# Cosine attention and a highway FFN: 112-row chunks scheduled by the framework, against 128-row lanes of three tokens in one fixed order

## The chip, the cores and the metric

One Trainium2 chip, one of its cores. The metric is the device time of one execution in microseconds (us). The engines are named as in the profile: PE (TensorE, matrix products; PEld its weight loads), DVE (VectorE), ACT (ScalarE), POOL (GpSimd), SP (SyncE, which here only issues DMAs). "PSUM" is the memory that PE writes, "SBUF" the working memory.

## The reference

Eight batches, twelve heads, 448 tokens, 64 elements per head. Attention with q and k divided by their norms, then a highway layer over the joined heads:

```python
q_n = q / (norm(q, axis=-1) + 1e-6);  k_n = k / (norm(k, axis=-1) + 1e-6)
scores = q_n @ k_n.T / tau                       # tau = 0.1; (8, 12, 448, 448)
attn = exp(scores - max) / (sum + 1e-9)
x = (attn @ v) as (8*448, 12*64) = (3584, 768)
H = maximum(x @ w_h, 0);  T = sigmoid(x @ w_t + b_t)     # w_h, w_t: 768 x 768
out = T * H + (1 - T) * x
```

All inputs and the output are float32.

## The kernel before

A batch has six pairs of neighbouring heads (2 pr, 2 pr + 1). The 448 tokens of a head lie on 112 partitions with four tokens each (chunk c = token 4p + c), so that all tiles have 112 rows.

*Norms and loads.* `emit_A` loads q and k of a pair (L92, 256-byte pieces, by SP), squares both on POOL (L97, 1024 elements a row) and sums them on DVE (L104). `emit_rsqrt` turns the sums into 1/norm on DVE by a bit trick and two Newton steps (L125 to L144): for batch 0 pair by pair, later once a batch.

*Transposes.* `emit_B` multiplies q and k by 1/norm on POOL (L152), transposes the eight 112 x 128 blocks on PE (L157), copies them out of PSUM on DVE (L164), loads v (L168) and casts it to fp16 on ACT (L174); a 65th column holds 2.0, so that the product with v also yields twice the sum of the exps.

*Scores.* `emit_qkt` computes k times q for two chunks of both heads (L186: contraction 64, the two heads in the upper and the lower half of the array), into two PSUM tiles of two banks each, and takes the exp of 896 elements at a time on ACT (L194) with the immediate scale 1/tau.

*Values.* `emit_av` multiplies exps with v: 16 products of 65 columns a head (L210), then a reciprocal and a scaling on DVE (L221, L222) into the batch's x tile, which so holds x/2.

*FFN.* For each quarter of the tokens `emit_xt` transposes x (L236) and copies it out (L242). `emit_ffn_quarter` runs six products of 384 columns (L257) for each half of w_h and of w_t, the bias as a seventh (L265), a tanh on ACT for the gate (L273), and max(H, 0) - x on DVE (L276). `emit_ffn_final` ends with two DVE operations a half (L293, L301) and a store (L309).

*Order.* The loops at the end of the kernel emit attention of batch b, FFN of batch b - 1 and the preparation of batch b + 1 interleaved; batch 0's preparation and the weights (L73, cast on DVE at L76) come first. The framework's scheduler places the instructions on the engines by these positions, with raised priority for the copies out of PSUM. All DMAs are issued by SP.

Of the kernel before, what the change touches and what calls it, by code (L numbers as in the profile page):

```python
# [15 lines left out]

@with_exitstack
def kernel(
# [12 lines left out]

    B, NH, S, D = q.shape
    P = 112
    NC = S // P
    NPAIR = NH // 2
    DM = NH * D
    CC = DM // 128
    MH = DM // 2
    inv_tau = 1.0 / float(tau)  # L40

    assert (B, NH, S, D) == (8, 12, 448, 64)

    const = ctx.enter_context(tc.tile_pool(name="const", bufs=1))
    wraw_p = ctx.enter_context(tc.tile_pool(name="wraw", bufs=1))
    qkraw_p = ctx.enter_context(tc.tile_pool(name="qkraw", bufs=7))
    qksq_p = ctx.enter_context(tc.tile_pool(name="qksq", bufs=3))
    nrm_p = ctx.enter_context(tc.tile_pool(name="nrm", bufs=2))
    qkn_p = ctx.enter_context(tc.tile_pool(name="qkn", bufs=4))
    qt_p = ctx.enter_context(tc.tile_pool(name="qt", bufs=4))  # L50
    vraw_p = ctx.enter_context(tc.tile_pool(name="vraw", bufs=3))
    vp_p = ctx.enter_context(tc.tile_pool(name="vp", bufs=4))
    expt_p = ctx.enter_context(tc.tile_pool(name="expt", bufs=4))
    xb_p = ctx.enter_context(tc.tile_pool(name="xb", bufs=2))
    xt_p = ctx.enter_context(tc.tile_pool(name="xt", bufs=2))
    ffns_p = ctx.enter_context(tc.tile_pool(name="ffns", bufs=4))
    outst_p = ctx.enter_context(tc.tile_pool(name="outst", bufs=4))

    sT_p = ctx.enter_context(tc.tile_pool(name="sTpool", bufs=2, space=bass.MemoryType.PSUM))
    pb1_p = ctx.enter_context(tc.tile_pool(name="pb1pool", bufs=2, space=bass.MemoryType.PSUM))  # L60
    ffnp_p = ctx.enter_context(tc.tile_pool(name="ffnpool", bufs=2, space=bass.MemoryType.PSUM))

    ident = const.tile([P, P], FP16)
    make_identity(nc, ident)
    w_h_f = const.tile([128, CC, DM], FP16)
    w_t_f = const.tile([128, CC, DM], FP16)
    bth = const.tile([128, DM], FP16)
    ones_row = const.tile([128, 128], FP16)

    def emit_weights():  # L70
        for w_src, w_dst in ((moe_w_h, w_h_f), (moe_w_t, w_t_f)):
            w_raw = wraw_p.tile([128, CC, DM], FP32, tag="wraw")
            nc.sync.dma_start(  # L73
                w_raw[:, :, :], w_src.rearrange("(cc p) m -> p cc m", p=128)
            )
            nc.vector.tensor_copy(w_dst[:, :, :], w_raw[:, :, :])  # L76

        bt_raw = wraw_p.tile([1, DM], FP32, tag="btraw")
        nc.sync.dma_start(bt_raw[:1, :], moe_b_t)
        nc.vector.memset(bth[:, :], 0.0)  # L80
        nc.vector.memset(ones_row[:, :], 0.0)
        nc.vector.tensor_single_scalar(bth[:1, :], bt_raw[:1, :], 0.5, ALU.mult)
        nc.vector.memset(ones_row[:1, :], 1.0)

    out_v = out.rearrange("(b p ic) m -> b ic p m", b=B, ic=NC)

    st = {}

    def emit_A(b, pr):
        qk_raw = qkraw_p.tile([128, 2, NC, 2, D], FP32, name="qk_raw")  # L90
        for t, src in enumerate((q, k)):
            nc.sync.dma_start(  # L92
                qk_raw[:P, t],
                src[b, 2 * pr : 2 * pr + 2].rearrange("h (p c) d -> p c h d", c=NC),
            )
        qk_sq = qksq_p.tile([128, 2, NC, 2, D], FP16, name="qk_sq")
        nc.gpsimd.tensor_mul(qk_sq[:P], qk_raw[:P], qk_raw[:P])  # L97

        if pr == 0:
            n2 = nrm_p.tile([128, NPAIR, 2, NC, 2], FP16, name="n2")  # L100
            st["n2", b] = n2
        n2 = st["n2", b]
        with nc.allow_low_precision(reason="norm^2 in fp16 (rel err 5e-4)"):
            nc.vector.reduce_sum(n2[:P, pr], qk_sq[:P], axis=AX.X)  # L104
        st["qk_raw", b, pr] = qk_raw

    def emit_rsqrt(b, prs=None):
        n2 = st["n2", b]
        NE = NPAIR * 2 * NC * 2
        if prs is None:  # L110
            if ("rs", b) not in st:
                st["rs", b] = nrm_p.tile([128, NE], FP32, name="yy")
            x32 = nrm_p.tile([128, NE], FP32, name="x32")
            yy = st["rs", b]
            tt_ = nrm_p.tile([128, NE], FP32, name="tt_")
            n2s = n2[:P].opt()
        else:
            if ("rs", b) not in st:
                st["rs", b] = nrm_p.tile([128, NE], FP32, name="yy")
            NE = 16  # L120
            x32 = nrm_p.tile([128, NE], FP32, name="x32p")
            yy = st["rs", b][:, prs * 16 : (prs + 1) * 16]
            tt_ = nrm_p.tile([128, NE], FP32, name="tt_p")
            n2s = n2[:P, prs].opt()
        nc.vector.tensor_copy(x32[:P], n2s)  # L125
        nc.vector.tensor_single_scalar(
            yy[:P].bitcast(I32), x32[:P].bitcast(I32), 1, ALU.arith_shift_right
        )
        nc.vector.tensor_scalar(
            out=yy[:P].bitcast(I32),  # L130
            in0=yy[:P].bitcast(I32),
            scalar1=-1.0,
            scalar2=float(0x5F3759DF),
            op0=ALU.mult,
            op1=ALU.add,
        )
        for _ in range(2):
            nc.vector.tensor_mul(tt_[:P], yy[:P], yy[:P])
            nc.vector.tensor_mul(tt_[:P], tt_[:P], x32[:P])
            nc.vector.tensor_scalar(  # L140
                out=tt_[:P], in0=tt_[:P], scalar1=-0.5, scalar2=1.5,
                op0=ALU.mult, op1=ALU.add,
            )
            nc.vector.tensor_mul(yy[:P], yy[:P], tt_[:P])  # L144

    def emit_B(b, pr):
        qk_raw = st.pop(("qk_raw", b, pr))
        rs = st["rs", b].rearrange("p (pr t c h) -> p pr t c h", pr=NPAIR, t=2, c=NC)
        qkn = qkn_p.tile([128, 2, NC, 2, D], FP16, name="qkn")
        for t in range(2):  # L150
            in1 = rs[:P, pr, t].unsqueeze(3).to_broadcast([P, NC, 2, D])
            nc.gpsimd.tensor_mul(qkn[:P, t], qk_raw[:P, t], in1)  # L152

        qkT = pb1_p.tile([128, 2, 512], FP16, name="qkT", tag="pb1")
        for t in range(2):
            for c in range(NC):
                nc.tensor.transpose(  # L157
                    qkT[:, t, c * P : (c + 1) * P],
                    qkn[:P, t, c],
                    ident[:P, :P],  # L160
                )
        qkt = qt_p.tile([128, 2, S], FP16, name="qkt")
        with tc.high_priority(offset=300):
            nc.vector.tensor_copy(qkt[:, :, :], qkT[:, :, 0:S])  # L164
        st["qkt", b, pr] = qkt

# [186 lines left out]
    for h in range(NH):  # L353
        ffn_slot(B - 1, h)
# [35 lines left out]
```

## Time and profile before

| what | value |
|---|---|
| median of three runs | 487.74 us |
| lowest, highest | 483.55, 488.44 us |
| span of the profiled execution | 485.1 us |
| instructions in it | 8592 |
| PE busy | 369.8 us (76%), 3328 matmuls |
| DVE busy | 309.2 us (64%) |
| ACT busy | 225.6 us (47%) |
| POOL busy | 206.4 us (43%) |
| mean granted PE clock | 0.903 |
| read from memory, written | 37.75 MB, 11.01 MB |
| DMA packets under 512 bytes | 131873 of 137034 |

The profile is of one execution; it lists its span from the first to the last instruction, and no device time of its own beside it. Busy time of PE counts each matmul from its start to its modelled end, so that matmuls that follow each other closely overlap. "Idle before, releaser" behind a group is the time for which its engine stood idle just before it, and the instruction that ended most of that. In the tables by stretch, the number in brackets is a count of instructions.

### The profile page before, as it was taken

The page shows a single profiled execution, that of the slowest core. Times are in us where ns is not written, and L with a number is a line of the kernel's source. Part 1 is how long each engine was busy: PE and PEld are TensorE (multiplying, and loading weights), DVE is VectorE, ACT ScalarE, POOL GpSimd, SP SyncE. Part 2 cuts the span into 40 slices and gives each one's busy share as a digit, 9 for nine tenths or more (in the row PEclk, how much of TensorE's full clock was granted, in tenths as well). Part 3 has the DMA queues.
Part 4 walks back from the last instruction along what each step waited for, and adds up shares of the span by engine and source line. Part 5 has one row for each costly group of instructions (what it writes and reads, how often), then busy time and mean ns, then how long its engine had stood idle before and what let it go on. Part 6 is the DMA issues. An engine that isn't in the chain of part 4 may idle for free.

```text
span 485.1 us, 8592 instructions
## 1 busy us (share of the span) xinstructions
PE 369.8 (76%) x3328; PEld 240.3 (50%) x3328; DVE 309.2 (64%) x661; ACT 225.6 (47%) x305; POOL 206.4 (43%) x294
## 2 busy tenths in 40 slices
PE   0553843796848777889887988887887999898995
PEld 0212502563425355556565655555555666465673
DVE  3656555458647787774978584858568555445674
ACT  2330632343525444644755473475356556645511
POOL 3663376833674175738363833374327122000000
PEclk9999999998978597876999797899789799789999
DMA  9980596941627335743663662356241122000122
GB/s 160 198 235 1 190 207 107 171 71 49 145 56 143 85 91 119 144 103 85 137 135 88 139 144 59 86 125 130 63 103 49 40 77 68 28 30 30 30 64 79
DMA packets 137034, 49.31 MB, mean 102 GB/s; under 512 B 131873, under 2 KB 131873, under 8 KB 136994
## 3 DMA queue, kind: packets, MB, share of 16 engines
q1 hardware_dynamic: 136994, 48.77, 46.2%
q8 instruction: 26, 0.43, 0.4%
q14 instruction: 14, 0.11, 0.1%
HBM read 37.75 MB, written 11.01 MB: 101 GB/s over the span
## 4 chain that ended last, share of the span: by engine, by line
PE 46%; DVE 24%; POOL 12%; ACT 6%; issue 6%; DMA 4%; SPq 0%; POOLq 0%; ACTq 0%
PE pt L257 24%; PE sT L186 9%; PE u L210 9%; POOL qkn L152 8%; DVE th1a L293 6%; DVE outst L301 5%; DVE n L104 5%; POOL qk_sq L97 5%; DMA qk_raw<-in_k_dram 4%; ACT expt L194 4%; PE qkT L157 3%; ACT tt L273 2%; DVE xTb L242 2%; PE pt L265 1%; DVE qkt L164 1%
## 5 line engine op out<-in xcount | busy, mean ns | idle before, releaser
L194 ACT ACTIVATE expt<-sT 112x896 f16<-112x896 f32 x192 | 166.2, 916 | 92.8 <-PE sT L186 73.2
L257 PEld LDWEIGHTS <-xTb 128*112 128x112 f16 x768 | 100.4, 143 | 58.7 <-DVE xTb L242 23.6
L186 PE MATMUL sT<-qkt 64*112 64x448 f16 x384 | 105.2, 434 | 25.8 <-ACT expt L194 25.1
L152 POOL TENSOR_TENSOR qkn<-qk_raw,yy 112x512 f16<-112x512 f32 x96 | 100.0, 1070 | 54.6 <-DVE yy L144 35.3
L257 PE MATMUL pt<-w_h_f,xTb 128*112 128x384 f16 x384 | 97.5, 394 | 14.4 <-DVE xTb L242 14.1
L97 POOL TENSOR_TENSOR qk_sq<-qk_raw 112x1024 f16<-112x1024 f32 x48 | 94.1, 1968 | 29.2 <-DMA qk_raw<-in_k_dram 21.7
L210 PEld LDWEIGHTS <-expt 112*128 112x128 f16 x1536 | 70.1, 108 | 46.2 <-issue 21.8
L210 PE MATMUL u<-vp,expt 112*128 112x65 f16 x1536 | 80.2, 210 | 16.1 <-DVE xbach L222 12.5
L104 DVE TENSOR_REDUCE n<-qk_sq 112x16 f16<-112x1024 f16 x48 | 58.1, 1212 | 40.6 <-POOL qk_sq L97 29.2
L257 PE MATMUL pt<-w_t_f,xTb 128*112 128x384 f16 x384 | 77.1, 329 | 3.3 <-DVE hmx L276 3.1
L174 ACT CAST vp<-v_raw 112x512 f16<-112x512 f32 x48 | 29.8, 621 | 99.3 <-PE u L210 81.5
L157 PE MATMUL qkT<-ident,qkn 112*128 112x112 f16 x384 | 35.2, 244 | 46.2 <-POOL qkn L152 43.6
L293 DVE SCALAR_TENSOR_TENSOR th1a<-tt,hmx 112x384 f16<-112x384 f16 x64 | 48.9, 764 | 28.6 <-ACT tt L273 28.3
L186 PEld LDWEIGHTS <-qkt 64*112 64x112 f16 x384 | 31.3, 140 | 63.1 <-issue 55.6
L273 ACT ACTIVATE tt<-pt 112x384 f16<-112x384 f32 x64 | 31.4, 491 | 61.6 <-PE pt L265 61.6
L276 DVE SCALAR_TENSOR_TENSOR hmx<-pt,xbach 112x384 f16<-112x384 f32 x64 | 35.2, 552 | 34.4 <-PE pt L257 34.4
L157 PEld LDWEIGHTS <-qkn 112*128 112x128 f16 x384 | 27.4, 113 | 57.0 <-POOL qkn L152 49.1
L340 POOL MEMSET expt<- 112x16 f16 x96 | 11.5, 126 | 102.6 <-PE u L210 65.8
L301 DVE SCALAR_TENSOR_TENSOR outst<-xbach,th1a 112x384 f32<-112x384 f16 x64 | 45.7, 715 | 1.0
L164 DVE COPY qkt<-qkT 128x896 f16<-128x896 f16 x48 | 29.8, 620 | 21.6 <-PE qkT L157 13.3
L222 DVE SCALAR_TENSOR_TENSOR xbach<-u,rd 112x256 f16<-112x256 f32 x96 | 40.2, 420 | 1.9
L221 DVE RECIPROCAL rd<-u 112x4 f32<-112x4 f32 x96 | 17.0, 177 | 28.5 <-PE u L210 28.5
(56 smaller groups left out, 125.0 us busy)
## 6 DMA issues: line engine op xcount, KB each, us to landing
qk_raw<-in_q_dram SPq DMA_DIRECT2D x48, 224.0 KB, 4.5
qk_raw<-in_k_dram SPq DMA_DIRECT2D x48, 224.0 KB, 4.7
v_raw<-in_v_dram SPq DMA_DIRECT2D x48, 224.0 KB, 3.7
out_dram<-outst SPq DMA_DIRECT2D x32, 336.0 KB, 2.9
w_raw<-in_moe_w_h_dram SPq DMA_DIRECT2D x1, 2304.0 KB, 10.1
w_raw<-in_moe_w_t_dram SPq DMA_DIRECT2D x1, 2304.0 KB, 9.2
bt_raw<-in_moe_b_t_dram SPq DMA_DIRECT2D x1, 3.0 KB
```

The lines of the kernel that those rows point to most:

```text
L97: nc.gpsimd.tensor_mul(qk_sq[:P], qk_raw[:P], qk_raw[:P])
L104: nc.vector.reduce_sum(n2[:P, pr], qk_sq[:P], axis=AX.X)
L152: nc.gpsimd.tensor_mul(qkn[:P, t], qk_raw[:P, t], in1)
L157: nc.tensor.transpose(qkT[:, t, c * P : (c + 1) * P], qkn[:P, t, c], ident[:P, :P],)
L186: nc.tensor.matmul(sTs[hh][:P, jj, 0:S], lhsT=qkt[hh * D : (hh + 1) * D, 1, jc * P : (jc + 1) * P], rhs=qkt[hh * D : (hh + 1) * D, 0, 0:S] ...
L194: nc.scalar.activation(st["expt", b, 2 * pr + hh][:P, 2 * g * S : (2 * g + 2) * S].rearrange("p (j s) -> p j s", j=2), sTs[hh][:P, :, 0:S] ...
L210: nc.tensor.matmul(u[:, ic, 0 : D + 1], lhsT=expt[:P, jc * S + ic * P : jc * S + ic * P + 128], rhs=vp[:P, jc, hh], start=(jc == 0), stop= ...
L222: nc.vector.scalar_tensor_tensor(out=xb[:P, pr, :, hh, :], in0=u[:P, :, 0:D], scalar=0.0, in1=rd[:P, :].unsqueeze(2).to_broadcast([P, NC, D]),
L257: nc.tensor.matmul(pt[:P, :], lhsT=xT[:, cc, ic * P : (ic + 1) * P], rhs=w_f[:, cc, mh * MH : (mh + 1) * MH], start=(cc == 0), stop=(cc == ...
L273: nc.scalar.activation(tt[:P, mh], pt[:P, :], AF.Tanh)
L293: nc.vector.scalar_tensor_tensor(out=th1a[:P, mh], in0=tt[:P, mh], scalar=1.0, in1=hmx[:P, mh], op0=ALU.add, op1=ALU.mult,)
L301: nc.vector.scalar_tensor_tensor(out=outst[:P, mh * MH : (mh + 1) * MH], in0=xg, scalar=2.0, in1=th1a[:P, mh], op0=ALU.mult, op1=ALU.add,)
```

## The change

The kernel is rewritten; the arithmetic is the same up to where factors are applied.

*Layout.* The first 384 tokens of a head lie on 128 partitions ("lanes") of three tokens each, and the last 64 are a tail. Heads n and n + 6 form a pair: their rows sit side by side, and their two tails (64 + 64 rows) share one 128-row tile.

*Loads.* q and k of a whole batch come in one DMA each, issued by POOL, which converts to fp16 on the way (1536 pieces of 768 bytes); the weights likewise. v, the tails and, for batch 0, the first two pairs (as float32) come by SP and ACT. Batch b + 1's loads stand in POOL's stream behind some q scalings of the batch before.

*Norms.* Squares on DVE in fp16, folded 64 to 32 to 16 by additions and then summed; Newton steps for a batch at once. Only q is multiplied by 1/norm (POOL). k is left unscaled: its 1/norm times 1/tau is a column of numbers, one for each partition, that the exp takes as its scale.

*Attention of a pair.* Nine transposes of 128 columns (three of q, three of k, two of q's tail, one of k's tail, laid out as a block diagonal of the two heads) into one PSUM bank, one copy of 1024 elements; six score products of 448 columns and six exps of 448; one product of 512 columns for the tail keys of both heads and one exp of 512; then 24 + 8 products of 65 columns, one reciprocal and one scaling of 448. The PSUM tiles are one bank each: four for scores (ring S), four for all else (ring B).

*FFN of a batch.* Three full tiles of 128 tokens, and a half tile with the 64 tails: its 64 rows are split over two column tiles of the array, the two halves of the 768 outputs side by side in one bank. Gate: tanh of half on ACT, gate scale and product on DVE in fp16, the final sum on POOL (on DVE for the last two tiles).

*Order.* Every operation is entered in a plan with assumed costs. A list `ORDER` of 1907 numbers is walked by `Plan.follow`, which gives each operation a start and its buffers; they are then emitted by start, and the framework keeps that order on each engine and adds the waits. Operations marked `port` (DVE products, copies in SBUF, POOL work) are kept apart in the plan only.

```diff
-        qk_sq = qksq_p.tile([128, 2, NC, 2, D], FP16, name="qk_sq")
-        nc.gpsimd.tensor_mul(qk_sq[:P], qk_raw[:P], qk_raw[:P])
...
-            nc.vector.reduce_sum(n2[:P, pr], qk_sq[:P], axis=AX.X)
...
-            nc.gpsimd.tensor_mul(qkn[:P, t], qk_raw[:P, t], in1)
...
-        for hh in range(2):
-            nc.scalar.activation(
-                st["expt", b, 2 * pr + hh][:P, 2 * g * S : (2 * g + 2) * S].rearrange(
-                    "p (j s) -> p j s", j=2
-                ),
-                sTs[hh][:P, :, 0:S],
-                AF.Exp,
-                scale=inv_tau,
-            )
...
+    NR = dict(qr=3, kr=3, qt=2, kt=2, kb=2, vr=2, vt=2, vp=2, sq=3, f1=2, f2=2, n2=2, rs=3, qn=3, kp=3,
+              qtn=2, qT=3, E=3, Et=3, rd=2, x=3, xT=3, tt=3, hm=3, gt=3, gg=3, os=4, S=4, B=4)
...
+    def main_src(t, b):
+        return t[b, :, 0 : 3 * 128, :].rearrange("h (l c) d -> l h (c d)", c=NCH)
...
+            if p1 - p0 == 6:
+                eng.dma_start(dst[:, :, :], main_src(src, b))
...
+                if onact:
+                    nc.scalar.activation(d, a, AF.Square)
+                else:
+                    nc.vector.tensor_mul(d, a, a)
...
+            lambda: nc.vector.tensor_add(v("f1"), v("sq")[:, :, :, 0:32], v("sq")[:, :, :, 32:64]),
+            lambda: nc.vector.tensor_add(v("f2"), v("f1")[:, :, :, 0:16], v("f1")[:, :, :, 16:32]),
+            lambda: nc.vector.reduce_sum(
...
+            nc.gpsimd.tensor_mul(
+                R("qn", s).rearrange("l c ab d -> l ab c d"),
+                rows(0, b, p, p + 1).rearrange("l ab (c d) -> l ab c d", c=NCH),
+                rcol(b, 0, p).unsqueeze(3).to_broadcast([128, 2, NCH, D]),
...
+            nc.vector.tensor_copy(R("kp", s).rearrange("l c ab d -> l ab c d"),
+                                  rows(1, b, p, p + 1).rearrange("l ab (c d) -> l ab c d", c=NCH))
...
+                for ab in range(2):
+                    qT = R("qT", s)[64 * ab : 64 * ab + 64]
+                    nc.tensor.matmul(R("S", 7 * s + 2 * c + ab)[:, 0:448],
+                                     lhsT=qT[:, 512 + 128 * c : 640 + 128 * c],
+                                     rhs=qT[:, 64 * (1 - ab) : 64 * (1 - ab) + 448],
+                                     start=True, stop=True)
...
+                    nc.scalar.activation(
+                        R("E", s)[:, c, 512 * ab : 512 * ab + 448], R("S", 7 * s + 2 * c + ab)[:, 0:448], AF.Exp,
+                        scale=rcol(b, 1, p)[:, ab, c : c + 1])
...
+                            for h in range(2):
+                                nc.tensor.matmul(
+                                    P[64 * h : 64 * h + 64, 0:MH],
+                                    lhsT=xT[:, cc % 3, 64 * (cc // 3) : 64 * (cc // 3) + 64],
+                                    rhs=w_[:, cc, MH * h : MH * h + MH], start=st, stop=(cc == CC - 1))
...
+        op("DVE", f"gt {g}", lambda: nc.vector.tensor_scalar(
+            out=R("gt", g)[:, 0:W], in0=R("tt", g)[:, 0:W], scalar1=0.5, scalar2=0.5, op0=ALU.mult, op1=ALU.add),
...
+        op("DVE", f"gg {g}", lambda: nc.vector.tensor_mul(
+            R("gg", g)[:, 0:W], R("gt", g)[:, 0:W], R("hm", g)[:, 0:W]), o, l, key + 0.3,
...
+        eng, en = (nc.vector, "DVE") if last else (nc.gpsimd, "POOL")
...
+        op(en, f"out {g}", lambda: eng.tensor_add(R("os", g)[:, 0:W], xall(), R("gg", g)[:, 0:W]), o, l, key + 0.3,
...
+    plan = pl.follow(ORDER)
+    with nc.allow_low_precision(reason="fp16 operands of the products, squares and gates as given"):
+        with tc.manual_schedule():
+            for o in plan:
+                o.fn()
```

How the six pairs of a batch are entered, with the keys that say where an operation belongs:

```python
for p in range(NP):
    s = base + p                  # base = 6 * b
    qnorm(b, p, s - 1.5)
    turn(b, p, s - 0.8)           # transposes, copy out of PSUM
    vcast(b, p, s - 0.5)
    scores(b, p, s)
    attend(b, p, s + 0.7)
for i in range(4):
    ffn(b, i, base + 7.0 + 1.6 * i)
```

856 lines of the change are left out of this document (581 added, 275 removed), and 78 rows, old and new, of the table ORDER.

## The prediction

> **What bounds the kernel now.** I read the page's head and its chain of waits first, then the table of stretches, cut where the FFN's first matmul starts (101 us) and where batch 7 has only its FFN and a few heads left (443 us).
>
> ```profile
> span 485.1 us, 8592 instructions
> ...
> PE 46%; DVE 24%; POOL 12%; ACT 6%; issue 6%; DMA 4%; SPq 0%; POOLq 0%; ACTq 0%
> ```
>
> ```profile
> core 0: us, PE busy (x) PEld busy (x) DVE busy (x) ACT busy (x) POOL busy (x), PEclk, DMA share, GB/s
> 0.00:101.00 101.00, 48.94 (x373) 26.96 (x374) 54.84 (x135) 33.58 (x41) 57.43 (x72) 1.00 0.84 159
> 101.00:443.00 342.00, 286.25 (x2662) 188.14 (x2660) 230.11 (x474) 178.73 (x244) 148.70 (x220) 0.87 0.39 91
> 443.00:485.00 42.00, 34.58 (x296) 25.23 (x294) 24.25 (x53) 13.31 (x21) 0.22 (x2) 0.98 0.17 53
> ```
>
> The chain has no single owner: it hops between PE, DVE and POOL. There are three regimes. In the first 101 us PE issues 373 of its 3328 matmuls; DMA (0.84) and POOL are the busy ones. In the middle 342 us (seven batches, 48.9 us each) PE shows 286 us busy, but that counts the latency of each matmul. What PE must really spend is the spacing of matmuls that stand queued. Four merged rows of the timeline show it:
>
> ```profile
> 251.23 0.83 PE L257 MATMUL pt<-w_t_f,xTb 128*112 128x384 f16 x4
> 252.06 0.56 PE L157 MATMUL qkT<-ident,qkn 112*128 112x112 f16 x8
> ...
> 252.92 0.67 PE L210 MATMUL u<-vp,expt 112*128 112x65 f16 x16
> 253.52 0.58 PE L186 MATMUL sT<-qkt 64*112 64x448 f16 x3
> ```
>
> Taking off the last one's own duration (0.33, 0.24, 0.21, 0.41) and dividing by the steps between starts gives 0.167 us for 384 columns, 0.046 for a transpose of 112, 0.031 for one of 65, and 0.09 for 448 columns where two half-height products run side by side. With the counts of the middle and of the end:
>
> ```profile
> L257 PE MATMUL pt<-w_h_f,xTb 128*112 128x384 f16 x313 | 84.1, 409 | 13.0 <-DVE xTb L242 12.7
> L186 PE MATMUL sT<-qkt 64*112 64x448 f16 x307 | 77.1, 409 | 19.5 <-ACT expt L194 18.9
> L257 PE MATMUL pt<-w_t_f,xTb 128*112 128x384 f16 x312 | 63.0, 330 | 2.9 <-DVE hmx L276 2.9
> L210 PE MATMUL u<-vp,expt 112*128 112x65 f16 x1234 | 61.9, 205 | 13.0 <-DVE xbach L222 9.4 <-DVE qkt L164 3.1
> L157 PE MATMUL qkT<-ident,qkn 112*128 112x112 f16 x288 | 22.6, 226 | 3.5 <-DVE xbach L222 2.7 <-POOL qkn L152 0.8
> L265 PE MATMUL pt<-bth,ones_row 128*112 128x384 f16 x52 | 17.0, 327 | 0.0
> L236 PE MATMUL xTp<-ident,xbach 112*128 112x112 f16 x156 | 13.6, 232 | 3.9 <-DVE qkt L164 3.9
> ```
>
> Middle: 677 x 0.167 + 307 x 0.09 + 1234 x 0.031 + 444 x 0.046 = 199 us of pure PE work in 342 us, 0.58. The rest is waits (right-hand columns: DVE's copies, ACT's exps) and a granted clock of 0.87.
>
> ```profile
> L257 PE MATMUL pt<-w_t_f,xTb 128*112 128x384 f16 x72 | 14.1, 328 | 0.4 <-DVE hmx L276 0.3
> L257 PE MATMUL pt<-w_h_f,xTb 128*112 128x384 f16 x72 | 13.8, 330 | 1.5 <-DVE xTb L242 1.4
> L210 PE MATMUL u<-vp,expt 112*128 112x65 f16 x94 | 4.2, 194 | 0.0
> L265 PE MATMUL pt<-bth,ones_row 128*112 128x384 f16 x12 | 3.9, 326 | 0.0
> L186 PE MATMUL sT<-qkt 64*112 64x448 f16 x16 | 3.5, 368 | 0.1
> L236 PE MATMUL xTp<-ident,xbach 112*128 112x112 f16 x30 | 2.1, 212 | 0.0
> ```
>
> End: 156 x 0.167 + 94 x 0.031 + 16 x 0.09 + 30 x 0.046 = 31.8 us in 42, 0.76, with a clock of 0.98. So the kernel is bound by how its queues interlock, not by one engine; the whole kernel holds about 249 us of PE work in a span of 485.
>
> **The change, part by part.** *PE.* Per pair of heads after: nine transposes of 128 columns (0.052 each, 0.47), six score products of 448 (0.54), one tail product of 512 (scaled from 0.167: 0.22), 32 products of 65 (0.98): 2.21 us. Per batch the FFN has three full tiles (6 transposes, 26 products: 4.65 each) and a half tile as two column tiles (13 pairs). No row shows column tiles: if they run side by side like the score halves, 2.3 us, if not 4.5; I take 2.3, the score rows being the nearest. A batch is 6 x 2.21 + 13.95 + 2.3 = 29.5 us, against 249/8 = 31 before. PE work falls by 5% only; the gain, if any, must come from packing.
>
> *DVE, ACT, POOL, per batch.* Their rows:
>
> ```profile
> L194 ACT ACTIVATE expt<-sT 112x896 f16<-112x896 f32 x192 | 166.2, 916 | 92.8 <-PE sT L186 73.2
> ...
> L152 POOL TENSOR_TENSOR qkn<-qk_raw,yy 112x512 f16<-112x512 f32 x96 | 100.0, 1070 | 54.6 <-DVE yy L144 35.3
> ...
> L293 DVE SCALAR_TENSOR_TENSOR th1a<-tt,hmx 112x384 f16<-112x384 f16 x64 | 48.9, 764 | 28.6 <-ACT tt L273 28.3
> ...
> L273 ACT ACTIVATE tt<-pt 112x384 f16<-112x384 f32 x64 | 31.4, 491 | 61.6 <-PE pt L265 61.6
> ...
> L164 DVE COPY qkt<-qkT 128x896 f16<-128x896 f16 x48 | 29.8, 620 | 21.6 <-PE qkT L157 13.3
> ```
>
> ```profile
> 239.62 3.43 ACT L194 ACTIVATE expt<-sT 112x896 f16<-112x896 f32 x4
> ```
>
> ```profile
> L293 DVE SCALAR_TENSOR_TENSOR th1a<-tt,hmx 112x384 f16<-112x384 f16 x12 | 6.7, 557 | 9.3 <-ACT tt L273 9.3
> ```
>
> The last row is th1a in the end stretch, where POOL is idle: 0.557 us for 384 elements, that is about 0.155 + 1.04 ns each. The copy of packed fp16 (0.620 for 896) is 0.155 + 0.52 ns. After, per batch: six copies of 1024 (4.1), six reciprocals and evictions of 448 (1.0 + 3.7), six k copies of 384 (2.1), seven hm (3.9), transposed-x copies (2.0), gate scale and product (2.0 + 2.0), squares (4 of 1152: 3.0), two folds and a short reduction (3.9), tail folds and k blocks (1.7), eight Newton steps (1.9): 31.3 us. The fp16 products are not in the trace; they lie between the copy's rate (taken: both are packed fp16) and th1a's, which adds 5.6. Removed are th1a, outst and the long reductions.
>
> POOL and DVE also hold each other up:
>
> ```profile
> 9.46 1.93 POOL L97 TENSOR_TENSOR qk_sq<-qk_raw 112x1024 f16<-112x1024 f32 x1 [1.70 <-DMA qk_raw<-in_k_dram]
> ```
>
> ```profile
> 9.67 1.75 DVE L138 TENSOR_TENSOR tt_p<-yy 112x16 f32<-112x16 f32 x1
> ```
>
> A 16-element product took 1.75 us: it ended with POOL's instruction. Over the run th1a pays 764 - 557 = 0.21 us for this. The new kernel has some 32 such operations a batch (products, SBUF copies), 6.4 us; POOL has about 13 us of work a batch (ten operations of 384 at 0.8, three of 768 at 1.6), as large a share of a shorter batch as now. The new planner keeps the two apart in its order, so I take 4.5 us, bounds 0 and 6.4. DVE: 35.8 us a batch.
>
> ACT: four exps of 896 start (3.43 - 0.916)/3 = 0.84 apart; from 916 and 491 an element is 0.83 ns, so 448 elements take 0.45 (0.08 fixed + 0.37). 36 of these, 6 tails of 512 (0.50), 7 tanh of 384 (0.40), 12 value casts of 192 (0.25), two of 384 (0.4): 25.8 us. The new exps take their scale per partition (k's norm); every exp row here has an immediate. Bounds 0 and 0.15 (a whole fixed part again), taken 0, as 25.8 hides under DVE. The Trainium skill (ScalarE: Activation LUTs, What ACT_TABLE_LOAD costs) adds about 93 ns for a pointer operand; by that ACT would reach 29.7 us a batch, still under DVE, and the start would grow by some 4 us, to 322 in all. No run so far shows it.
>
> *Start.* All loads share the DMA engines, whose best slice moved 235 GB/s:
>
> ```profile
> GB/s 160 198 235 1 190 207 107 171 71 49 145 56 143 85 91 119 144 103 85 137 135 88 139 144 59 86 125 130 63 103 49 40 77 68 28 30 30 30 64 79
> ```
>
> In the new ACT queue the fourteen value casts of batch 0 stand ahead of the first exp, so it waits for v: 3.93 MB (first pairs, tails, other q and k, v) at 235 is 17 us + 1.5 to start, + 3.8 for the casts: first exp at 22 us. Six steps at ACT's pace (7 exps, 3.3 us): 42. Batch 1's q and k queue on POOL behind the weights: 11.6 MB, 51 us; squares, Newton, q scaling, transposes: 58 us. Batch 0's FFN (16 us of PE) fills 42 to 58, its weights being in at 39. The old kernel starts its first FFN at 101.
>
> *Middle and end.* 42 steps and seven FFN: per batch DVE needs 35.8 us, PE 29.5. PE at the density of the old end stretch (0.76 of 42 us, or 31.8/36.4 = 0.87 up to its last matmul; mean 0.82) would need 36.0. Both give 36: 252 us. Then the last gate, product and sum on DVE (three operations like th1a, 1.7 us) and a store: 5 us in all, an estimate. 58 + 252 + 5 = 315 us of span, against 485.1; the median run is 487.74, 2.6 above that span, so 318.
>
> Of the other parts: the converting q and k loads leave SP for POOL's queue, ahead of q scalings there, and their issue may hold POOL (rival 3). The removed expt and vp memsets were POOL's, which is idle more than half of the middle; they count nothing.
>
> **Rivals.** (1) *PE alone sets the middle*: the order hides DVE's locks, 29.5 x 7 = 207: 58 + 207 + 5 + 2.6 = 273, up to 300 with small gaps. For it: 31.3 is DVE without locks, with full latencies counted. Chance 0.20. (2) *The queues interlock as badly as now*, density 0.58: 29.5/0.58 = 51 us a batch, 422. For it: one fixed order over five queues stalls whenever a step runs later than planned. Against: the old waits are for double exps and paired buffers, which are cut in half. 0.10. (3) *POOL's loads hold POOL*: issue as long as the transfer, 2.36 MB at 235, 10 us a batch, of which q buffers for three steps cover part; I put 8 us a batch on the path: 318 + 56 = 374. The Trainium skill (SBUF — State Buffer, Who interferes with whom) has DVE's two-port operations block descriptor generation on POOL, which would do this; the lock row above agrees for arithmetic, no row for loads. 0.10. (4) *Slower*: converting loads crawl. 23.6 MB (q, k and weights) pass there; below 49 GB/s (23.6 MB in 480 us) nothing else matters, and at 45 the time is 524 + 27 = 551. Against: the old transfers averaged 91 to 159 GB/s in these stretches with smaller pieces. 0.04. (5) Gains eaten evenly, no change: 0.02.
>
> **The numbers.** Forecast (300 to 340) 0.54. The range leaves out rival 2, half of rival 1 and the last two: 280 to 385. A measurement of this kernel tells about 1% from no change; faster by more 0.94, within 0.02, slower 0.04.
>
> **What would show it.** First exp near 22 us and batch 1's first score product near 58; DVE the busiest engine by share, over 0.8 in the middle; PE's granted clock near 1 there; two-input DVE operations lengthened by 0.1 to 0.2 us. PE waiting for qn or DVE for a POOL load speaks for rival 3; a middle of 30 us a batch for rival 1; first exp after 30 us would make the start wrong.

## The result and the profile after

The changed kernel takes 338.97 us (median of four runs, 337.8 to 341.14) against 488.09 for the kernel before on the same chip: a ratio of 0.697, 95% interval 0.691 to 0.702. (A ratio is estimated without executions more than 1.5% above the fastest of their kernel, and so need not be the quotient of the medians shown.) The profiled execution has a span of 336.6 us. First the head of its page, the chain of waits, and the table of stretches, cut at batch 1's first score product (73.8 us) and at the last eviction of attention (313.7 us):

```profile
span 336.6 us, 8281 instructions
...
PE 286.0 (85%) x3304; PEld 176.4 (52%) x3304; DVE 247.4 (73%) x598; ACT 241.2 (72%) x508; POOL 126.0 (37%) x128
...
PE 35%; ACT 27%; issue 12%; DVE 11%; DMA 8%; POOL 4%; SPq 3%; POOLq 0%; DVEq 0%; ACTq 0%
```

```profile
0.00:73.80 73.80, 43.21 (x424) 25.25 (x425) 50.18 (x156) 37.30 (x83) 27.21 (x36) 0.97 0.94 170
73.80:313.70 239.90, 225.54 (x2747) 140.55 (x2749) 185.28 (x418) 200.06 (x417) 91.42 (x89) 0.97 0.47 96
313.70:336.60 22.90, 17.22 (x139) 10.58 (x135) 11.90 (x26) 3.88 (x8) 7.41 (x5) 0.97 0.29 104
```

The columns are the stretch, its length, then busy time and instructions of PE, weight load, DVE, ACT and POOL, the granted clock, the DMA share and GB/s. POOL, which held 12% of the chain, holds 4% now; ACT has gone from 6% to 27%. In the middle ACT is busy for 200.06 of 239.9 us (0.83), DVE for 0.77, and PE, by latencies, for 0.94 at a clock of 0.97.

The middle came out near its forecast, the start did not. From the first score of batch 1 to the end are 262.8 us (forecast 252 + 5), and that score itself came at 73.8 us (forecast 58). Two timelines of the changed kernel show how; columns are start, length, engine and work. On ACT:

```profile
21.21 2.74 ACT L633 ACTIVATE E<-pS,rs 128x448 f16<-128x448 f32 x5 [0.28 <-PE pS L624]
...
42.39 3.41 ACT L633 ACTIVATE E<-pS,rs 128x448 f16<-128x448 f32 x6
```

The first exp starts at 21.2 us. From 31.9 us on batch 0's exps run back to back, but not 0.45 us apart: six in 3.41 us, one of which lasts 0.65, are 0.55 apart. On DVE and PE, after batch 0's attention:

```profile
49.30 1.49 DVE L746 COPY xT<-pB 128x768 f16<-128x768 f16 x3 [0.49 <-PE pB L741]
...
59.85 0.36 DVE L801 TENSOR_SCALAR gt<-tt 128x768 f16<-128x768 f16 x1 [2.77 <-ACT tt L787]
60.54 0.56 DVE L794 SCALAR_TENSOR_TENSOR hm<-pB,x 128x384 f16<-128x384 f32 x1 [0.32 <-PE pB L775]
61.01 1.42 DVE L462 TENSOR_TENSOR sq<-kr 128x1152 f16<-128x1152 f16 x2
...
67.11 1.27 DVE L536 SCALAR_TENSOR_TENSOR rs<-rs,n 128x84 f32<-128x84 f32 x1
...
70.05 0.20 DVE L540 TENSOR_SCALAR rs<-rs 128x84 f32<-128x84 f32 x1
```

```profile
71.00 0.29 PE L601 MATMUL pB<-ident,qtn 128*128 128x128 f16 x1 [4.88 <-POOL qtn L574]
...
73.79 0.93 PE L624 MATMUL pS<-qT 64*128 64x448 f16 x4 [0.85 <-DVE qT L615]
```

Batch 1's k squares stand on DVE behind the first pieces of batch 0's FFN and start at 61.0. From there to the first score are 12.8 us of squares, folds, Newton steps, q's scaling on POOL and transposes. PE waits in it for 4.9 us before the first transpose and again for 0.9 before the score. When k was there, the lines of k's tile say (the two loads of k issued between 20 and 40 us):

```profile
L373 POOL DMA_DIRECT2D kr<-in_k_dram x2: 1017/1017/1017, 23.7 to 35.1; - x2
...
DMA to landing us min/median/max: 23.2/24.3/25.5
```

The load of batch 1 was issued at 23.7 and took 25.5 us: k had landed by 49.2. So 73.8 = 49.2 + 11.8 (k waits for its place on DVE) + 12.8 (the chain). In the 11.8 us DVE's timeline has gaps of 0.93, 0.15, 2.77 and 0.32 us: for 4.2 us DVE does nothing, and the fixed order still puts other work first. The 12.8 hold pieces of the FFN too, and a Newton product of 1.27 us (it takes 0.25 the second time) beside a sum of POOL, which runs from 66.65 to 68.29.

### The profile page after: what moved, and what is told of

It is laid out like the page before. It is cut to its first block, busy times and chain, and to the rows that moved or that the text cites. A ratio compares the mean times of both kernels' runs of the same rounds, so it can differ in the third digit from the quotient of the medians.

```text
span 336.6 us, 8281 instructions
## 1 busy us (share of the span) xinstructions
PE 286.0 (85%) x3304; PEld 176.4 (52%) x3304; DVE 247.4 (73%) x598; ACT 241.2 (72%) x508; POOL 126.0 (37%) x128
## 3 DMA queue, kind: packets, MB, share of 16 engines
q1 hardware_dynamic: 37154, 25.57, 28.5%
## 4 chain that ended last, share of the span: by engine, by line
PE 35%; ACT 27%; issue 12%; DVE 11%; DMA 8%; POOL 4%; SPq 3%; POOLq 0%; DVEq 0%; ACTq 0%
ACT E L633 18%; PE pB L775 14%; PE pS L624 5%; DMA vr<-in_v_dram 4%; PE pB L682 4%; ACT Et L648 4%; ACT vp L658 3%; DMA f<-in_q_dram 2%; PE pB L770 2%; ACT tt L787 2%; DMA kt<-in_k_dram 2%; PE pB L679 2%; SPq L393 2%; PE pB L698 2%; DVE qT L615 2%
## 5 line engine op out<-in xcount | busy, mean ns | idle before, releaser
L633 ACT ACTIVATE E<-pS,rs 128x448 f16<-128x448 f32 x288 | 166.9, 697 | 31.0 <-PE pS L624 28.8
L811 POOL TENSOR_TENSOR os<-x,gg 128x768 f32<-128x768 f16 (+1 forms) x30 | 45.2, 1509 | 131.8 <-DVE gg L805 131.8
L775 PEld LDWEIGHTS <-xT 128*128 128x128 f16 x576 | 52.4, 98 | 39.4 <-issue 10.9
L624 PE MATMUL pS<-qT 64*128 64x448 f16 x288 | 55.2, 372 | 9.3 <-DVE qT L615 3.4
L775 PE MATMUL pB<-wt,xT 128*128 128x384 f16 x288 | 62.1, 328 | 0.0
L775 PE MATMUL pB<-wh,xT 128*128 128x384 f16 x288 | 60.3, 328 | 1.6 <-DVE qT L615 1.0
L682 PE MATMUL pB<-vp,E 128*128 128x65 f16 x864 | 51.2, 197 | 0.7 <-ACT E L633 0.4
L562 POOL TENSOR_TENSOR qn<-qr,rs 128x384 f16<-128x384 f16 x46 | 40.0, 882 | 26.7 <-PE pB L603 20.8
L794 DVE SCALAR_TENSOR_TENSOR hm<-pB,x 128x384 f16<-128x384 f32 x56 | 30.9, 553 | 22.2 <-PE pB L775 19.5
L679 PE MATMUL pB<-vp,Et 128*128 128x65 f16 x288 | 44.5, 196 | 1.9 <-ACT Et L648 1.8
L682 PEld LDWEIGHTS <-E 128*128 128x128 f16 x864 | 41.1, 100 | 4.5 <-ACT E L633 1.4
L679 PEld LDWEIGHTS <-Et 128*128 128x128 f16 x288 | 28.5, 99 | 18.0 <-issue 12.3
L648 ACT ACTIVATE Et<-pS,rs 128x512 f16<-128x512 f32 x48 | 36.5, 760 | 0.8 <-PE pS L642 0.7
L712 DVE RECIPROCAL rd<-pB 128x7 f32<-128x7 f32 x48 | 9.6, 200 | 21.0 <-PE pB L682 12.3
L801 DVE TENSOR_SCALAR gt<-tt 128x768 f16<-128x768 f16 (+1 forms) x32 | 11.8, 368 | 14.2 <-ACT tt L787 14.1
## 6 DMA issues: line engine op xcount, KB each, us to landing
kr<-in_k_dram POOLq DMA_DIRECT2D x7, 576.0 KB, 14.6
```

The costliest lines, as they stand in the source:

```text
L562: nc.gpsimd.tensor_mul(R("qn", s).rearrange("l c ab d -> l ab c d"), rows(0, b, p, p + 1).rearrange("l ab (c d) -> l ab c d", c=NCH), rcol ...
L624: nc.tensor.matmul(R("S", 7 * s + 2 * c + ab)[:, 0:448], lhsT=qT[:, 512 + 128 * c : 640 + 128 * c], rhs=qT[:, 64 * (1 - ab) : 64 * (1 - ab ...
L633: nc.scalar.activation(R("E", s)[:, c, 512 * ab : 512 * ab + 448], R("S", 7 * s + 2 * c + ab)[:, 0:448], AF.Exp, scale=rcol(b, 1, p)[:, ab ...
L648: op("ACT", f"exp {s} t", lambda: nc.scalar.activation(R("Et", s)[:, 64:576], R("S", 7 * s + 6)[:, :], AF.Exp, scale=R("rs", b)[:, 3, 78 + ...
L679: nc.tensor.matmul(U[:, 2 * c + ab, :], lhsT=Et[:, 128 + 128 * c : 256 + 128 * c], rhs=vp[:, 6 + ab, :], start=True, stop=False)
L682: nc.tensor.matmul(U[:, 2 * c + ab, :], lhsT=E[:, j, 576 * ab + 128 * c : 576 * ab + 128 * c + 128], rhs=vp[:, 3 * ab + j, :], start=False ...
```

## The experiments

The runs were made on three chips, on which the kernel before took 486.5 to 489.4 us at the median; ratios are to the kernel before on the same chip. All compare with the changed kernel (339.0 us; "the stretch" is from batch 1's first score to the last eviction of attention, 239.9 us there). Columns: median and ratio to the kernel before with its interval, then first score, last eviction and span of the profiled execution.

| run | us | ratio | first score | last eviction | span |
|---|---|---|---|---|---|
| changed kernel | 339.0 | 0.697 (0.691 to 0.702) | 73.8 | 313.7 | 336.6 |
| x1 immediate scales | 325.6 | 0.667 (0.663 to 0.670) | 70.3 | 300.7 | 323.6 |
| x2 POOL only fills | 336.2 | 0.689 (0.685 to 0.693) | 81.7 | 311.8 | 335.0 |
| x3 loads and norms moved | 342.3 | 0.702 (0.699 to 0.705) | 78.9 | 318.8 | 341.7 |
| x4 v by POOL's loads | 369.0 | 0.755 (0.751 to 0.759) | 88.3 | 344.6 | 367.5 |
| x5 half the FFN's products | 329.4 | 0.676 (0.671 to 0.682) | 71.8 | 308.8 | 327.9 |
| x6 new order | 344.9 | 0.701 (0.691 to 0.711) | 80.9 | 323.8 | 346.5 |
| x7 k scaled on POOL | 338.2 | 0.692 (0.683 to 0.702) | 78.8 | 311.0 | 334.7 |
| x8 new order, engines kept apart | 326.7 | 0.670 (0.667 to 0.673) | 76.5 | 301.8 | 324.6 |
| x9 x7 in such an order | 334.8 | 0.683 (0.678 to 0.689) | 77.8 | 309.3 | 332.1 |
| x10 x1 and x2 together | 310.4 | 0.636 (0.633 to 0.639) | 69.5 | 285.8 | 308.7 |
| x11 as x8, k's landing as measured | 317.6 | 0.652 (0.647 to 0.656) | 67.2 | 292.2 | 315.0 |
| x12 as x11, weights loaded later | 322.7 | 0.663 (0.658 to 0.668) | 64.7 | 300.2 | 323.0 |

**What the scale column costs.** Both exps of a pair (L633, L648) change:

```
-   AF.Exp, scale=rcol(b, 1, p)[:, ab, c : c + 1])
+   AF.Exp, scale=0.125 * inv_tau)
```

> All 336 exps take the immediate scale 1/(8 tau) in place of a column of scales; k's norm is left out of the scores, all else is as in the changed kernel (338.97 us). Theory A, ACT sets the middle together with DVE: the exps come 0.45 us apart instead of 0.546, ACT's busy time falls by about 336 x 0.093 = 31 us, and the time falls by 10 to 25 us, to 314 to 329. Theory B, DVE and PE set the middle and ACT only waits beside them: ACT's busy time falls as much, the time by no more than 4 us, the first batch's attention (3.7 us a step, ACT alone) included.

The group of the exps in x1, and ACT's timeline at the same place of batch 0:

```profile
L633 ACT ACTIVATE E<-pS x288: 523/552/685, 21.0 to 297.1; 128x448 f16<-128x448 f32 x144
```

```profile
36.64 2.76 ACT L633 ACTIVATE E<-pS 128x448 f16<-128x448 f32 x6
```

An exp takes 552 ns at the median, against 652 in the changed kernel's group (row below); six take 2.76 us, not 3.41. ACT's busy time falls by 27.4 us (241.2 to 213.8), the time by 13.4. In the profiled spans 3.5 us of it come before batch 1's first score and 9.5 in the stretch. Theory A holds: ACT was not covered by DVE.

```profile
L633 ACT ACTIVATE E<-pS,rs x288: 623/652/1071, 21.2 to 310.2; 128x448 f16<-128x448 f32 x144
```

The Trainium skill (ScalarE: Activation LUTs, What ACT_TABLE_LOAD costs) puts a pointer operand at about 93 ns; the two medians are 100 ns apart, so the trace agrees.

**What POOL costs DVE.** The two products of `qnorm` and `qtnorm`, the tails' squares and the final sums become fills:

```
-   nc.gpsimd.tensor_mul(R("qn", s)..., rows(0, b, p, p + 1)..., rcol(b, 0, p)...)
+   nc.gpsimd.memset(R("qn", s)[:, :, :, :], 0.125)
...
-   nc.gpsimd.tensor_mul(sq, a, a)
+   nc.gpsimd.memset(sq, 0.01)
```

> POOL's two-input products (q's norm, the tails' squares, the final sum of x and the gated part of all but the last two tiles) become fills of the same size, so q's norm, the tails' squares and that sum are left out. Theory A, DVE is lengthened by POOL through the port that they share, and DVE sets the middle: DVE's products of two inputs fall back to about 0.25 us (rs), 0.35 us (folds) and 0.75 us (squares), its busy time falls by 15 to 25 us, and the time falls by 8 to 20 us. Theory B, the overlap is a matter of DVE's own operand types and costs nothing on the path: DVE's busy time falls by less than 5 us or the time by less than 3 us.

DVE's busy time falls from 247.4 to 230.1 us: squares of q from 0.829 to 0.750, the Newton products from 0.443 and 0.423 to 0.232, the tails' first fold from 0.687 to 0.347. The squares in the changed kernel, then in x2 (mean ns behind the bar):

```profile
L462 DVE TENSOR_TENSOR sq<-qr 128x1152 f16<-128x1152 f16 x15 | 12.3, 829 | 0.0
```

```profile
L462 DVE TENSOR_TENSOR sq<-qr 128x1152 f16<-128x1152 f16 x15 | 11.1, 750 | 0.0
...
L536 DVE SCALAR_TENSOR_TENSOR rs<-rs,n 128x84 f32<-128x84 f32 x14 | 3.3, 232 | 0.1
```

The time falls by 2.8 only, because the start is another one: POOL's fills wait for no norms, so that the weights' loads go out at 7.2 us, not 17.2, ahead of much of v, and ACT's value casts wait for v until 28.5 us, not 16.8. The first eviction comes at 39.2 us, not 28.7. The stretch is 9.8 us shorter. DVE's busy time fell as theory A has it, the time by less than 3 us as theory B has it; the run supports theory A for the middle and says nothing on the whole. The fills also halve POOL's own work (126.0 to 68.2 us) and need no norms. That was not tested apart from the lock; in the changed kernel's stretch PE's idle times are put down to POOL for 0.3 us, those of its weight loads for 3.9. x10 repeats the fills from batch 1 on, with POOL's products of batch 0 left as they were.

**Batch 1's chain first.** The loads of the weights go behind batch 1's loads of q and k, and batch 1's norms ahead of batch 0's FFN on DVE, q's scaling ahead of its sums on POOL:

```
+   plan = after(plan, {"ld wt", "ld wh"}, "ld kr 1 0")
...
+   plan = move(plan, norms, "cpx 0")
+   plan = move(plan, {"qtn 1", "qn 1 0", "qn 1 1", "qn 1 2"}, "out 0")
```

> The whole is computed. The weights' two loads are issued behind batch 1's loads of q and k; batch 1's squares, folds and Newton steps stand on DVE ahead of the first copy of batch 0's FFN, and q's norm of batch 1 on POOL ahead of the first sum of that FFN. Theory A, the late second batch (first score at 73.8 us instead of the 58 forecast) is a matter of the hand-written order: batch 1's scores now start between 58 and 66 us, the idle PE of 66 to 73.8 us goes, and the time falls by 7 to 12 us, to 327 to 332. Theory B, the loads set it: the first score stays behind 70 us, the time within 3 us of 339.

Slower by 3.3 us: theory A misses, and theory B by its bound of 3 us. The norms were ready early, and the score did not follow:

```profile
50.65 1.42 DVE L462 TENSOR_TENSOR sq<-kr 128x1152 f16<-128x1152 f16 x2
...
57.45 0.20 DVE L540 TENSOR_SCALAR rs<-rs 128x84 f32<-128x84 f32 x1
57.57 1.48 DVE L746 COPY xT<-pB 128x768 f16<-128x768 f16 x3
```

The last Newton step is done at 57.7, not 70.3; but PE's own order still has the transposes of batch 1 behind the whole FFN, which now starts 8 us later and slowly: after 8.4 us of idleness its first six products take 2.10 us, not 1.14. With no FFN piece between them, k's squares to the last Newton step take 7.0 us here, against 9.2 in the changed kernel. The loads do not set the late score; moving work on one engine did not help while the order of the others stood.

**Less for ACT by other means.** The 112 value casts (96 of pairs, 16 of tails) go; POOL loads v straight into the tile of 65 columns:

```
-   nc.scalar.copy(dst[:, ab], src[:, ab])
...
+   nc.gpsimd.dma_start(t_vp[b % 3][:, :, 3 * ab + c, 0:D], v[b, 6 * ab : 6 * ab + 6, ...])
```

> The whole is computed. v is loaded by POOL's converting DMAs straight into the tile of 65 columns (eight a batch), and ACT's 98 value casts go. Theory A, ACT sets the pace together with DVE: ACT's busy time falls by 35 us, the time by 12 to 30 us, to 309 to 327. Theory B, DVE and PE set the pace: the time falls by no more than 5 us, by what the first exp comes earlier. Theory C, POOL is held by its eight more DMAs a batch (issue of about 1 us each and waits for older ones): q's norm comes late, PE waits for it, and the time does not fall or rises.

ACT's busy time falls by 29 us and the kernel takes 30 us more: theory C. POOL's timeline in batch 0, and PE's:

```profile
37.88 0.83 POOL L872 DMA_DIRECT2D vp<-in_v_dram x1 [5.93 <-DMA wh<-in_moe_w_h_dram]
40.15 0.82 POOL L872 DMA_DIRECT2D vp<-in_v_dram x1 [1.43 <-DMA qr<-in_q_dram]
43.25 0.66 POOL L875 DMA_DIRECT2D vp<-in_v_dram x1 [2.28 <-DMA kr<-in_k_dram]
```

```profile
44.82 0.50 PE L601 MATMUL pB<-ident,qn 128*128 128x128 f16 x3 [11.99 <-POOL qn L560]
```

To issue one takes up to 0.86 us, and POOL's busy time rises by 49 us (126.0 to 175.2). POOL also waits for older transfers before it issues the next, 5.93 us for a weight; q's scaling stands behind, and PE is idle for 12 us. The stretch is 16 us longer as well (256.3).

**Less for PE.** The contraction of the FFN runs over three of its six pieces:

```
    for cc in range(lo, hi):
+       if cc in (1, 2, 3):
+           continue
```

> The FFN's products take three of the six pieces of the contraction (the pieces 1, 2 and 3 are left out); every other instruction is as in the changed kernel. PE loses 288 products of 0.21 us busy and 96 of the half tiles, some 60 us of 286. Theory A, PE alone sets the middle (the prediction's first rival): the middle falls from 36.8 us a batch to what DVE (30.9) and ACT (30.2) need, and the time by 35 us or more, to 304 or less. Theory B, PE, DVE and ACT wait for each other in turn in an order that fits none of them: the time falls by 8 to 25 us. Theory C, PE is covered: by less than 5 us.

```profile
PE 243.7 (74%) x2920; PEld 144.8 (44%) x2920; DVE 248.1 (76%) x598; ACT 241.3 (74%) x508; POOL 126.0 (38%) x128
```

PE's busy time falls by 42 us (286.0 to 243.7; 60 were expected), the time by 9.5. Of the 8.7 us in the profiled spans the stretch gives 2.9, the end after the last eviction 3.8 and the start 2.0. PE alone does not set the middle. By the size of the total it is theory B, by that of the stretch almost C.

**A new order.** Nothing but the list of steps changes; it is worked out again with the planner's model of engines, rings and loads, and durations from the trace:

```
+   if k == 'exp': o.occ, o.lat = (546, 546 + 215) if n[2] != 't' else (600, 600 + 215)
+   elif k == 'vc': o.occ, o.lat = 640, 640 + 170
...
+       o.port = False
```

> The whole is computed, by the same instructions; only their order on each engine is worked out anew, with this trace's durations for those of the plan (an exp takes ACT 0.546 us where the plan has 0.425, a pair of value casts 0.62 where it has 0.43, DVE's pieces by the rows of the trace, loads 235 GB/s). Summed with those durations the engines need 250 us (DVE), 249 (ACT) and 238 (PE). Theory A, the order loses what lies between those and 339 us: the time falls by 17 to 28 us, to 311 to 322. Theory B, the engines slow each other (ports, clock) and the order matters little: the time stays within 5 us of 339, or is longer, since the new order is as hand-fast as the old.

Its four runs lie between 339.5 and 348.2 us, none below the changed kernel's median; the profile is of the longest. The gain that the sum of busy times promised did not come: theory B. The last line of the edit is the reason to look at: it lets POOL's products stand beside DVE's. DVE's busy time rose from 247.4 to 267.0 us:

```profile
L497 DVE TENSOR_TENSOR sq<-kr 128x1152 f16<-128x1152 f16 x15 | 16.7, 1120 | 0.0
...
L510 DVE TENSOR_REDUCE n<-f 128x36 f32<-128x576 f16 x15 | 11.2, 749 | 0.4
```

The squares of k take 1.12 us, which took 0.75 beside fills; the reduction with its one input takes the same 0.74 to 0.75 in every run. In x7, which allows the overlap too and gives POOL more work, the squares take 1.14 (q) and 1.05 (k).

**A new order, engines kept apart.** As x6, but DVE's fast copies and products and POOL's products exclude each other in the plan, with the durations of x2 for DVE; the first 228 steps stand as in the changed kernel.

> The whole is computed, by the same instructions; the first 228 steps stand as in the changed kernel, the rest is put in a new order by the trace's durations, and no product of POOL stands beside a fast copy or product of DVE in it (in the run with the new order alone they did, and DVE's busy time rose from 247 to 267 us). Theory A, that overlap is what the new order lost by: DVE's busy time comes back to 247 us or less, and the time falls by 10 to 24 us under the changed kernel's, to 315 to 329. Theory B, the slack between the engines' 250 us and 339 is needed by waits that no such order takes in: DVE's time falls, the time stays at 335 or above.

326.7 us, theory A: DVE's busy time is 245.4 us and the stretch 225.3, 14.6 shorter than in the changed kernel with the same instructions. Three things differ from x6 (the exclusion, DVE's durations, the start), so what the exclusion alone is worth was not measured. Where the plan's times slip, the lock still shows. DVE and POOL in batch 0's FFN:

```profile
60.90 4.30 DVE L510 TENSOR_TENSOR sq<-kr 128x1152 f16<-128x1152 f16 x2
```

```profile
60.59 4.00 POOL L859 TENSOR_TENSOR os<-x,gg 128x768 f32<-128x768 f16 x2 [23.35 <-DVE gg L853]
```

Two squares that take 1.42 us alone take 4.30 beside two of POOL's sums, which take 4.00 in place of some 3.2 (1.64 each in the changed kernel).

**k's norm back into k.** x7 scales k on POOL, as q, in place of DVE's copy, and all exps take the immediate 1/tau; x9 leaves the tails as they are and keeps the engines apart:

```
-   nc.vector.tensor_copy(R("kp", s)..., rows(1, b, p, p + 1)...)
+   nc.gpsimd.tensor_mul(R("kp", s)..., rows(1, b, p, p + 1)..., rcol(b, 1, p)...)
```

> The whole is computed. k's norm goes back into k: POOL multiplies k by its column as it does q (48 products of 0.88 us), DVE's 48 plain copies of k go, all exps take the immediate scale 1/tau, and the order is worked out anew with the trace's durations. By these ACT needs 218 us, DVE 234, PE 238, POOL 170. Theory A, ACT's scale column (0.093 us an exp) costs more than POOL's second product: the time comes to 300 to 314 us and under that of the run with the new order alone by 4 to 12 us. Theory B, POOL becomes the late one (PE waits for q and k from it, or DVE is lengthened by it): the time is no less than that of the new order alone.

> The whole is computed. As in the run with k's norm on POOL, but the tails keep their plain copy and their column of scales (the scaled copies of the tails took DVE 1.21 us each there), and the order keeps POOL's products away from DVE's fast pieces. Theory A, less ACT (288 exps 0.093 us shorter) and less DVE (48 copies) win: 312 to 328 us. Theory B, POOL's 42 us more, which lock DVE out wherever they are put, take it back: 332 us or more, and DVE's squares stay above 0.9 us.

x7 takes 338.2 us, x9 334.8: ACT is down to 215.1 and 220.8 us of busy time, POOL up to 177.0 and 172.0. x9 is 8 us slower than x8, the same kind of order without this: theory B. x9's squares of q take 1.04 us, of k 0.97, and DVE is busy for 250.6 us, more than x8's 245.4 although 48 copies of k are gone from it: DVE loses to POOL what ACT gains. x7 fits neither theory: its median is 6.7 us under x6's, with intervals that overlap, and far above theory A's 300 to 314.

**ACT and DVE both relieved.** x1 and x2 in one kernel, in the changed kernel's order.

> The order of the changed kernel; the exps take an immediate scale (k's norm is left out of the scores), and from batch 1 on POOL's products are fills (q's norm, the tails' squares and the final sum are left out there; batch 0 keeps them, so that the start stays as it was). From the first to the last eviction of a U tile the changed kernel needs 285.0 us, the immediate scales alone 272.7, the fills alone 272.6. Theory A, ACT and DVE both hold the path, in different places: the two add up, that stretch falls to 258 to 265 us and the time to 312 to 319. Theory B, they hold it in the same places: 268 to 273, and 322 to 327. Theory C, PE is next at once: as B, with PE busy 19.5 of 20 us or more in every window of the middle.

310.4 us. The evictions of the changed kernel, then of x10:

```profile
L715 DVE SCALAR_TENSOR_TENSOR x<-pB,rd x48: 609/623/626, 28.7 to 313.7; 128x448 f16<-128x448 f32 x48
```

```profile
L721 DVE SCALAR_TENSOR_TENSOR x<-pB,rd x48: 605/624/625, 29.0 to 285.8; 128x448 f16<-128x448 f32 x48
```

From the first to the last are 256.8 us, 28.2 less than in the changed kernel, where the two alone gave 12.3 and 12.4 (their own first to last evictions): they add up and a little more (theory A, beyond its range). The window of 100 to 280 us of the changed kernel, then of x10:

```profile
100.00:280.00 180.00, 169.13 (x2039) 105.03 (x2035) 147.68 (x329) 150.00 (x322) 74.18 (x71) 0.98 0.52 106
```

```profile
100.00:280.00 180.00, 179.27 (x2280) 114.79 (x2276) 141.60 (x344) 142.50 (x340) 42.61 (x78) 1.00 0.56 121
```

PE gets 2280 matmuls through in place of 2039 and shows hardly a gap: busy, with latencies, for 179.27 of 180 us. PE looks like the next bound; no run took work from it in this kernel, so that is not shown.

**The late second batch, mended.** The plan of x8 believed that batch 1's k lands at 61 us. x11 is ordered for a landing by 51; x12 also has the weights' loads behind batch 1's, as x3.

> The whole is computed, by the same instructions. As in the run whose order keeps POOL's products apart from DVE's fast pieces, but the plan is now told that batch 1's k has landed by 51 us (the changed kernel's trace: 49.2; the plan before it believed 61), so batch 1's squares and Newton steps stand on DVE as soon as k is there, and PE's turn of its first pair ahead of batch 0's last half tile. Theory A, the late second batch (first score at 73.8 us, forecast 58) is a matter of order: the first score comes between 62 and 68 us, the first eviction of batch 1 before 78 (85.3 in the run before), and the time falls under the 326.7 of that run, to 313 to 321. Theory B, batch 0's FFN or POOL holds the chain wherever it stands: the first score stays behind 70 us and the time at 324 or more.

> As the run with batch 1's chain on k's landing, with the weights' two loads behind batch 1's loads of q and k as well, and batch 0's FFN spread over batch 1's steps, since its weights come later. Theory A, the loads' order is worth nothing once the work is ordered for it (FFN waits instead of the scores): first score between 58 and 64 us, the time within 3 us of the other run's. Theory B, earlier scores count: 3 to 8 us under it. Theory C, the late weights hold up PE, as they did where the weights were moved without the order (342.3): 5 us or more above it.

Theory A: x11 takes 317.6 us, 0.652 of the kernel before (0.647 to 0.656) and below the changed kernel's interval: the fastest that computes the whole. DVE and PE in batch 0's FFN:

```profile
54.38 1.42 DVE L510 TENSOR_TENSOR sq<-kr 128x1152 f16<-128x1152 f16 x2
```

```profile
67.17 0.55 PE L672 MATMUL pS<-qT 64*128 64x448 f16 x4
67.65 0.66 PE L823 MATMUL pB<-wt,xT 128*128 128x384 f16 x3
```

k's squares start 6.6 us earlier, the first score comes at 67.2, and FFN products stand ahead of the chain's transposes and behind that score: PE's 4.9 us of waiting are gone. The stretch is 225.0 us, as in x8, and all of the gain over it lies ahead (76.5 to 67.2). DVE's busy time is 247.6 us, that of the changed kernel, so the 21 us come from where the work stands and not from less of it. x12's first score comes at 64.7, its time is 5.1 us longer than x11's: theory C. Its PE is busy for 13.5 of the 20 us from 40 to 60, at a clock of 0.74 (x11: 14.7 at 0.91), and its stretch is 235.5 us.

## Why the prediction was right, and where not

The forecast was 318 us and the range 280 to 385; 339 came out. Of the 21.6 us by which the span exceeds the forecast 315, 15.8 had built up by batch 1's first score, and 5.8 came behind it.

*Start, first exp: right.* 22 us forecast, 21.2 measured: v was there at 16.8 (forecast 18.5), the fourteen casts took 4.1 (3.8), and ACT then waited 0.28 for the first scores.

*Start, batch 0's attention: mis-sized.* 42 us forecast, 48.8 measured (last eviction 48.2 + 0.6). The exps' scale column was taken as free, "bounds 0 and 0.15"; it is 0.10 us an exp. x1's last eviction of batch 0 comes at 44.7, so this term is 3.5 of the 6.8 us. The rest has two parts that the sum left out: ACT waits 2.9 us for scores in the first three steps, and the last values and eviction end 1.9 us after the last exp (46.9). The Trainium skill's rule (ScalarE: Activation LUTs, What ACT_TABLE_LOAD costs), cited beside that term, would have given "some 4 us" for the scale column.

*Start, first score of batch 1: the step that failed.* The prediction had batch 0's FFN fill 42 to 58 us while the norms of batch 1 run beside it: landing at 51, and 7 us for squares, Newton, scaling and transposes. Landing was right (49.2). The chain is 12.8 us long (61.0 to 73.8; and 54.4 to 67.2 in x11), and it does not run beside the FFN: the order has it behind FFN pieces on DVE for 11.8 us, and has more of them within it. The 7 us are too short even without these: in x3 squares to Newton alone took 7.0, and from the last Newton step to the score are 3.5 more in the changed kernel (70.3 to 73.8). x11 shows that 6.6 of the 11.8 are the order's. The rest was not settled: no run brought the score to 58, and x3 and x12 show that to bring loads and norms forward costs elsewhere.

*Middle: right in size, wrong in what it was made of.* 262.8 us to the end against 257. The prediction had DVE set it with 35.8 us a batch, "as 25.8 hides under DVE" for ACT. By busy time DVE needs 30.9 a batch (247.4/8), with a lock of 2.2 (17.3/8, x2) in place of 4.5; ACT needs 30.2 (241.2/8). DVE's term was 5 us too large, and ACT's 4.4 too small but not in the sum; by DVE alone the middle would have been shorter. The size was kept by the other estimate, that PE works as densely as at the end of the old kernel; that DVE's term gave the same 36 us a batch was luck. Neither engine sets the middle alone: take 27 us from ACT and the stretch falls by 9.5, free DVE from POOL and it falls by 9.8, do both and it falls by 23.6 (239.9 to 216.3), while 42 us less of PE gives 2.9. ACT and DVE take turns in holding a fixed order back; x8, an order made with measured durations and the engines kept apart, gained 14.6 there with the same instructions. The estimate of PE's density, 0.82, came true all the same: between the first and the last eviction of batches 1 to 7 (82.8 to 313.7 us) lie 41 steps and about six FFN, by the prediction's PE terms 41 x 2.21 + 6 x 16.25 = 188 us in 230.9, or 0.81.

*What would show it.* "DVE the busiest engine by share, over 0.8 in the middle" was wrong: DVE has 0.77, ACT 0.83 (and PE, with latencies, 0.94). PE's clock near 1 was right (0.97). Two-input operations were lengthened, the squares of q by less than the 0.1 to 0.2 us forecast (0.829 against 0.750), Newton products by that (0.443 against 0.232), the tails' fold by more.

*Rivals.* (1) PE alone: refuted by x5; x10, with ACT's and DVE's holds taken away, comes nearest to it: 207 us for the same 41 steps, where PE's terms give 188 (0.91). (2) As badly interlocked as before, 422 us: refuted by the time; but x6 shows that an order can lose what the sum of work promises. (3) POOL held by its loads: a load of k costs POOL 1.02 us to issue (the row above), not as long as its transfer, so not in this kernel; eight more a batch held POOL in x4, by waits for older transfers. (4) Crawling loads: refuted, k of batch 1 came in 25.5 us. (5) No change: refuted.

## What to carry to other kernels

A fixed order is only as good as the durations it was made with: when a profile shows other ones, work the order out again, with what the engines cost each other in it; here that was worth 21 us of 339 with the same instructions, while new durations without that (x6) gained nothing. When several engines are each busy for 0.75 to 0.85 of a stretch, ask what each gives back when it is relieved alone and in pairs, because sums of busy time neither bound the time from above nor name the one that holds it. Put two-input work of POOL where DVE does reductions, PSUM reads or nothing.

## What the runs showed of the hardware

The overlap of POOL and DVE gained nothing where it was seen: beside two of POOL's sums two squares took 4.30 us, not 1.42, and the sums 4.00, not some 3.2. Together they last from 60.59 to 65.20, 4.6 us, about as long as one after the other would (1.42 + 3.2). DVE was busy for 20 us more in a plan that allows the overlap (x6), and for 17.3 less with fills in place of POOL's products (x2). The reduction (0.74 to 0.75 us) and the evictions from PSUM (0.62 us) were the same in every run. The Trainium skill (SBUF — State Buffer, Who interferes with whom) has DVE's instructions with two inputs in SBUF contend with a POOL instruction that reads SBUF and not with one that only writes, and reductions not at all; these rows agree.

Two products of a half tile on two halves of PE's columns do run side by side, as the prediction took it. In the changed kernel's timeline

```profile
64.85 0.68 PE L770 MATMUL pB<-wh,xT 128*64 128x384 f16 x6
```

six take 0.68 us of which the last takes 0.33, so 0.07 us each, or 0.14 a pair, against 0.167 for a full one.
